# A GEGLU block by seven-product multiplication: one gate/up product of units 6 to 11 divided once more over unit pairs and passes

## Chip, cores, metric

The kernel runs on one core of one Trainium2 chip. The metric is the device time of one execution in microseconds; lower is better. A profile of one execution shows what each engine did: TensorE (PE for its matmuls, PEld for its weight loads), VectorE (DVE), ScalarE (ACT), GpSimd (POOL), and SyncE (SP), which issues the DMAs.

## The reference

```python
# x (1, 2048, 1024), w_gate and w_up (1024, 3584), w_down (3584, 1024), all bfloat16
g = einsum("bsd,df->bsf", x, w_gate)
u = einsum("bsd,df->bsf", x, w_up)
h = gelu(g, approximate=True) * u
return einsum("bsf,fd->bsd", h, w_down)
```

## The kernel before

The 2048 rows of x are worked in two passes (`NPASS`) of two chunks of N = 512 rows. A pass first computes h for its 1024 rows (gate/up stage), then multiplies by `w_down` (`down`). Both products are done by the seven-product scheme of Strassen and Winograd on 2x2 blocks: sums of blocks are formed beforehand, seven block products in place of eight are run on TensorE, and the results are added.

**The gate/up stage** runs over `NU` = 14 units. A unit u holds 256 columns of both `w_gate` and `w_up`, split into two blocks of 128 (fb = 2u and 2u + 1). The contraction of 1024 is split into halves of four blocks of 128 (`KH`), the rows of the pass into the two chunks. The sums of x (`t1` to `t4`, and `tb`, a cast) are made by VectorE once a pass, as fp32r tiles of 128x512. The sums of the weights (`s1` to `s4`) are made by GpSimd in `make_s`, one unit or more ahead of their use; `sa` and `tb` are casts by ScalarE. The seven products of a unit, each for gate and up, each of 4 matmuls of 128x128 by 128x512: two with the raw bf16 weights (`raw_products`, P1 and the one for c11) and five in fp32r, in `unit`: s2 t2, s1 t1, s3 t3, s4 tb and **A22 T4** (`s["sa"]`, `t["t4"]`, last). The raw products of two units are run together near the end of each odd unit, so that TensorE changes between bf16 and fp32r once a pair.

**Banks.** The eight PSUM banks of 128x512 fp32 are used in pairs (gate, up), called E, K, C, F before. The pair e of a unit collects P1, then s2 t2, s3 t3 and A22 T4; between them ScalarE copies its state out (`snap`, p1 and u2). d takes s1 t1 (copied out as p5) and s4 tb. The third pair is scratch: in pass 0 `keep_part` forms there, with ScalarE and VectorE, a part of the sums of `w_down` that the down stage needs (`m`, a pool of one buffer, stored to DRAM by `store_made`). VectorE adds the parts (`add`, `sum`), ScalarE applies `gelu`, VectorE multiplies into `hT` (`times`). `finish_raw` does this for the block that the raw products give.

**Order.** The instructions of SP, VectorE, GpSimd and TensorE, and in these stages of ScalarE, run in program order on each engine; an engine that waits holds up all that stands behind it on that engine. In `unit` the helper `aside` marks places at which other work is put: `aside(0)` stands behind s2 t2 and issues the load of the weights of unit u + 2; `after_p5` (`prepare`) stands behind s1 t1 and its copies, ahead of s3 t3: it makes the next unit's sums on GpSimd, stores the finished `m` and fetches `w_down` rows (`fetch_wd`); `aside(1)` stands ahead of the last additions.

**Buffers.** All small tiles (sums, copies, gelu results, w_down rows) share one pool of 52 slots of 2 KB a partition (`kpool`). The weights of a unit take one of three `w` buffers. The x of a pass takes `xT0` and `xT1`, one buffer each.

All additions appear in the profile under a helper's line: L91 for VectorE (`dve`), L94 for GpSimd (`pool`), L112 for all matmuls; L108 is `snap`, L103 `cast`, L180 `gelu`, L272 the copy in `keep_part`. Names of tiles tell them apart: `m<-bank` is `keep_part`, `sum<-bank,p` and `bank<-bank,p` are the additions of p5 or p1, `sum<-bank,u` those of u2, `hT<-g,bank` is `times`.

Of the kernel before, what the change touches and what calls it, by code (L numbers as in the profile page):

```python
# [10 lines left out]
def kernel(  # L11
# [39 lines left out]
    NKB = Dm // P  # L51
# [31 lines left out]
    def slot(shape, dtype, name):  # L83
        return kpool.tile(shape, dtype, name=name, tag="k")
# [5 lines left out]
    def dve(out, a, b, op):  # L90
        nc.vector.tensor_tensor(out=out, in0=a, in1=b, op=op)  # L91
# [4 lines left out]
    def new(eng, a, b, op, name, shape=None, dtype=None):  # L96
        t = slot(shape or [P, N], dtype or f32r, name)
        eng(t, a, b, op)
        return t

    def cast(src, name, shape=None):
        t = slot(shape or [P, N], f32r, name)
        nc.scalar.copy(out=t, in_=src)  # L103
        return t

    def snap(ps, name):
        t = slot([P, N], f32, name)
        nc.scalar.copy(out=t, in_=ps)  # L108
        return t
# [40 lines left out]
    def sums_s(w, eng):  # L150
        GU = range(2)
        sh = [P, KH, P]
        a11, a21 = [[w[:, i, :KH, h : h + P] for i in GU] for h in (0, P)]
        a12, a22 = [[w[:, i, KH:, h : h + P] for i in GU] for h in (0, P)]
        return Sums(
            how={
                "s1": lambda q, GU=GU: [new(eng, a21[i], a22[i], ADD, "s1", sh) for i in GU],
                "s2": lambda q: [new(eng, q["s1"][i], a11[i], SUB, "s2", sh) for i in GU],
                "s3": lambda q: [new(eng, a11[i], a21[i], SUB, "s3", sh) for i in GU],
                "s4": lambda q: [new(eng, a12[i], q["s2"][i], SUB, "s4", sh) for i in GU],  # L160
                "sa": lambda q: [cast(a22[i], "sa", sh) for i in GU],
            }
        )

    def pool_behind(tile):
        nc.gpsimd.tensor_copy(out=seen, in_=tile[:, :1].bitcast(f32))
# [3 lines left out]
        t.make("t1", "t2", "t3", "tb", "t4")  # L170
        return t

    def make_s(w, eng):
        s = sums_s(w, eng)
        s.make("s1", "s2", "s3", "sa", "s4")
        return s

    def gelu(src):
        g = slot([P, N], f32, "g")
        nc.scalar.activation(g, src, ACT.Gelu_apprx_tanh)  # L180
        return g

    def times(fb, c, g, u):
        dve(hT[:, fb // NJ, fb % NJ, c, :], g, u, MUL)

    def product(ps, lhs, rhs, start):
        for k in range(KH):
            matmul(ps, lhs[:, k, :], rhs[k], start and k == 0, k == KH - 1)

    def raw_products(e, c, xT, w):  # L190
        for i in range(2):
            product(e[i], w[:, i, :KH, :P], [xT[0][:, k, :] for k in range(KH)], True)
        p1 = [snap(e[i], "p1") for i in range(2)]
        for i in range(2):
            b21 = [xT[0][:, KH + k, :] for k in range(KH)]
            product(c[i], w[:, i, KH:, :P], b21, True)
        return p1

    def add(ps, other):
# [4 lines left out]
    def finish_raw(u, c, p1):  # L204
        g, up = add(c, p1)
        times(2 * u, 0, gelu(g), up)

    def unit(u, banks, s, t, late, after_p5, aside, keep, ahead_of_p4, behind_p4):
# [19 lines left out]
        after_p5()  # L228
        for i in GU:
            product(e[i], s["s3"][i], t["t3"], False)  # L230
        g, up = new(dve, e[0], p5[0], ADD, "sum", dtype=f32), banks[1][not late]
        dve(up, e[1], p5[1], ADD)
        if late:
            times(2 * u, 0, *c11)
        for i in GU:
            product(c[i], s["s4"][i], t["tb"], False)
        times(2 * u + 1, 1, gelu(g), up)
        aside(1)
        g, up = add(c, u2)
        times(2 * u, 1, gelu(g), up)  # L240
        ahead_of_p4()
        for i in GU:
            product(e[i], s["sa"][i], t["t4"], False)
        behind_p4()
        times(2 * u + 1, 0, gelu(e[0]), e[1])

    td = dpool.tile([P, NJ, 3, N], f32, name="td")  # L250
    wraw, made = {}, {}

    def fetch_wd(js):
# [381 lines left out]
    E, K, C, F = odd, cc, dd, even  # L635

    def loaded(u):
        if u not in ws:
            ws[u] = load_w(u)
        return ws[u]  # L640

    def raw_of(u, e):
        p1 = raw_products(e, K, xT, loaded(u))
        return lambda: finish_raw(u, K, p1)

    for ip in range(NPASS):
        with tc.manual_schedule(engines={ENG.Activation}):
            if ip == 0:
                ws = {1: w, 2: ahead}
                late = lambda: add(cc, nxt["p1"])  # L650
            else:
                raw_of(0, F)()
                raw_of(1, C)()
            for u in range(1 if ip == 0 else 0, NU):
                js = making(u) if ip == 0 else []
                first = (ip, u) == (0, 1)

                def prepare():
# [23 lines left out]
                def ahead_of_p4():  # L682
                    if u % 2 and u + 1 < NU:
                        raw_of(u + 1, F)()
                        nxt["c11"] = raw_of(u + 2, C)

                def behind_p4():
                    if "c11" in nxt:
                        nxt.pop("c11")()

                if u % 2 and not first:
                    E, K, C = C, E, K
                banks = (E, K, C) if u % 2 else (F, K, E)
                unit(
                    u, banks, s, t, late if first else None, prepare, aside, keep,
                    ahead_of_p4, behind_p4,
                )
                s = nxt.pop("s", None)
# [22 lines left out]
        down(ip, F + K, C + E, last, more)  # L721
        E, K, C, F = K, E, F, C
        if not last:
            t, s = got["t"], got["s"]

# [28 lines left out]
```

## Time and profile before

| | |
|---|---|
| median of 3 runs | 539.94 us (539.25 to 540.3) |
| profiled execution | 539.29 us, span 537.5 us |
| granted TensorE clock, mean | 0.999 |
| TensorE busy | 532.7 us, 2451 matmuls |
| VectorE busy | 356.3 us, 536 instructions |
| ScalarE busy | 258.1 us, 457 instructions |
| GpSimd busy | 259.3 us, 243 instructions |
| the sums of weights on GpSimd, `s<-w` alone | 102 of 1188 ns |

The span is the time from the first to the last instruction of the profiled execution; the execution's own time is 1.8 us longer. Shares of busy time are averages over the whole span, and TensorE's busy time counts its pipelined matmuls from start to end, so the step from one matmul's start to the next says more than a row's duration.

### The profile page before, as it was taken

What the parts mean: (1) busy time and instruction counts of PE and PEld (TensorE: products, weight loads), DVE (VectorE), ACT (ScalarE), POOL (GpSimd) and SP (SyncE); (2) the same over time, 40 slices, a digit from 0 to 9 for tenths busy, and PEclk for the clock granted to TensorE, in tenths of its full rate; (3) what the DMA queues carried; (4) which work ended last, traced back from release to release, by engine and by line L of the source; (5) the groups of instructions that cost most, each with busy time, mean ns of one, the idle gap of its engine ahead of it and who ended that gap; (6) DMA issues with size and microseconds to landing.
All of it is one profiled execution on the core that took longest, in us unless ns stands there. A gap on an engine that the chain in (4) does not pass through costs nothing.

```text
span 537.5 us, 7573 instructions
## 1 busy us (share of the span) xinstructions
PE 532.7 (99%) x2451; PEld 382.4 (71%) x2451; DVE 356.3 (66%) x536; ACT 258.1 (48%) x457; POOL 259.3 (48%) x243
## 2 busy tenths in 40 slices
PE   8999999999999999999999999999999999999997
PEld 4568686867777746888868677776868685478887
DVE  2986766767676894595855464555554639979844
ACT  2556675666666410265355555555555551113340
POOL 1179966677773500000087767676766600000194
PEclk9999999999999999999999999999999999999999
DMA  9675666759482999999873233242520049573752
GB/s 245 156 186 168 186 177 176 218 136 262 131 234 71 383 357 298 308 197 275 264 187 88 78 80 81 77 119 50 145 57 23 2 130 390 204 236 88 243 169 70
DMA packets 108199, 93.30 MB, mean 174 GB/s; under 512 B 17280, under 2 KB 93056, under 8 KB 108160
## 3 DMA queue, kind: packets, MB, share of 16 engines
q1 hardware_dynamic: 108160, 92.82, 59.6%
q8 instruction: 20, 0.33, 0.3%
q14 instruction: 19, 0.16, 0.1%
HBM read 74.45 MB, written 15.20 MB: 167 GB/s over the span
## 4 chain that ended last, share of the span: by engine, by line
PE 98%; DMA 1%; SPq 0%; DVE 0%; issue 0%
PE bank L112 98%; DMA xn<-in_x_dram 1%; SPq L538 0%; DVE st L91 0%; PE bank L545 0%
## 5 line engine op out<-in xcount | busy, mean ns | idle before, releaser
L94 POOL TENSOR_TENSOR s<-w 128x512 fp32r<-128x512 bf16 x102 | 119.0, 1188 | 163.0 <-PE bank L112 113.5
L112 PE MATMUL bank<-t,s 128*128 128x512 f32 x648 | 151.7, 390 | 0.0
L112 PEld LDWEIGHTS bank<-t,s 128*128 128x128 f32 x648 | 121.7, 188 | 25.4
L112 PE MATMUL bank<-xT,w 128*128 128x512 bf16 (+1 forms) x504 | 109.7, 376 | 0.0
L108 ACT COPY p<-bank 128x512 f32<-128x512 f32 x124 | 69.8, 590 | 45.2 <-PE bank L112 45.1
L91 DVE TENSOR_TENSOR sum<-bank,p 128x512 f32<-128x512 f32 x54 | 37.3, 691 | 79.4 <-PE bank L112 78.3
L112 PEld LDWEIGHTS <-w 128*128 128x128 bf16 x504 | 48.1, 98 | 58.1 <-issue 3.4
L91 DVE TENSOR_TENSOR hT<-g,bank 128x512 bf16<-128x512 f32 x112 | 76.8, 688 | 17.6 <-PE bank L112 4.5
L180 ACT ACTIVATE g<-sum 128x512 f32<-128x512 f32 x81 | 51.4, 635 | 74.5 <-DVE sum L91 74.2
L94 POOL TENSOR_TENSOR q<-q 128x256 fp32r<-128x256 f32 x28 | 21.1, 788 | 80.0 <-PE bank L112 79.4
L112 PE MATMUL bank<-q 128*128 128x512 f32 x240 | 59.0, 389 | 0.0
L94 POOL TENSOR_TENSOR s<-w,s 128x512 fp32r<-128x512 bf16 x50 | 57.7, 1175 | 0.0
L94 POOL TENSOR_TENSOR s<-s,w 128x512 fp32r<-128x512 f32 x50 | 57.2, 1166 | 0.0
L112 PE MATMUL bank<-t,sa 128*128 128x512 f32 x216 | 55.9, 401 | 0.0
L112 PE MATMUL bank<-tb,s 128*128 128x512 f32 x216 | 53.3, 389 | 0.0
L108 ACT COPY u<-bank 128x512 f32<-128x512 f32 x62 | 35.5, 589 | 34.3 <-PE bank L112 34.2
L112 PEld LDWEIGHTS bank<-q 128*128 128x128 f32 x240 | 45.1, 188 | 9.3
L112 PE MATMUL bank<-raw,hT 128*128 128x512 bf16 x224 | 48.7, 379 | 0.0
L112 PEld LDWEIGHTS bank<-t,sa 128*128 128x128 f32 x216 | 40.6, 188 | 9.4
L103 ACT CAST tb<-raw 128x512 fp32r<-128x512 bf16 x28 | 17.2, 624 | 62.6 <-DMA raw<-in_w_down_dram 34.1
L112 PEld LDWEIGHTS bank<-tb,s 128*128 128x128 f32 x216 | 40.6, 188 | 8.4
L91 DVE TENSOR_TENSOR bank<-bank,p 128x512 f32<-128x512 f32 x54 | 37.7, 699 | 8.8 <-PE bank L112 6.2
(60 smaller groups left out, 493.8 us busy)
## 6 DMA issues: line engine op xcount, KB each, us to landing
raw<-in_w_down_dram SPq DMA_DIRECT2D x76, 256.0 KB, 5.1
q<-td SPq DMA_DIRECT2D x60, 256.0 KB, 4.9
w<-in_w_gate_dram SPq DMA_DIRECT2D x27, 512.0 KB, 5.9
w<-in_w_up_dram SPq DMA_DIRECT2D x27, 512.0 KB, 7.0
td<-m SPq DMA_DIRECT2D x12, 768.0 KB, 4.6
w<-td SPq DMA_DIRECT2D x6, 1024.0 KB, 10.1
out_dram<-st SPq DMA_DIRECT2D x32, 128.0 KB, 1.7
td<-w SPq DMA_DIRECT2D x2, 768.0 KB, 6.3
```

The source lines that it names most:

```text
L91: nc.vector.tensor_tensor(out=out, in0=a, in1=b, op=op)
L94: nc.gpsimd.tensor_tensor(out=out, in0=a, in1=b, op=op)
L103: nc.scalar.copy(out=t, in_=src)
L108: nc.scalar.copy(out=t, in_=ps)
L112: nc.tensor.matmul(ps, lhsT=lhs, rhs=rhs, start=start, stop=stop, skip_group_check=True)
L180: nc.scalar.activation(g, src, ACT.Gelu_apprx_tanh)
```

## The change

For units 6 to 11, taken as pairs (6, 7), (8, 9), (10, 11) (`SPLIT`), A22 T4 is no longer computed whole in each unit and pass. The A22 of both units of a pair make one matrix, its rows halved by unit and its contraction halved into two blocks of two; the T4 of pass 0 and that of pass 1 make the other. This 2x2 by 2x2 product is done once more by seven products (of 2 x 2 matmuls for gate and up) in place of eight. Five of them run in pass 0, in the odd unit (`split_first`); two of their results are stored to DRAM (`dz`). Two run in pass 1, also in the odd unit (`split_second`), and the stored parts are added there.

What this needs:
- GpSimd makes three extra sums of weights for a pair in each pass (`split_sums`): in pass 0 in the odd unit's `prepare`, ahead of the next unit's sums, in pass 1 in the even unit's, behind them. ScalarE casts A22 only in pass 0 and in the unit itself (`sa` of the even unit, half of it, `sh`, of the odd one).
- T4 of pass 1 has to be there in pass 0. The x of pass 1 is loaded in units 1 and 3 (`NEXT_X`, 16 transposing DMAs in all) into a part of `hT` that is written only from unit 10 on, and VectorE forms 18 sums of 128x512: four times three for T4 (`next_t4`), twice three for the sums of both T4 (`inner_i`). The table `PREP` says how many of them are issued where: "0" at `aside(0)`, "p" at the end of `prepare`, "1" at `aside(1)`. Part of T4 is stored (`di`) and loaded again in unit 1 of pass 1 (`load_i1`).
- The bank pairs get other roles (Ea, Eb, K, D). In a split pair both units keep their e until the end; D is taken three times by half products in pass 0, with copies by ScalarE in between.
- In an odd split unit `up` goes to a slot instead of a bank. `fetch_wd` moves from the end of `prepare` to its beginning, in most split units to `aside(0)`. The raw products of a split pair are issued as two first ones and then two second ones in pass 0.

```diff
+    SPLIT = (6, 8, 10)
+    NEXT_X = {1: (0, 2), 3: (1, 3)}
+    PREP = {(2, "p"): 1, (2, "1"): 1, (3, "0"): 1, (3, "p"): 2, (3, "1"): 1, (4, "0"): 1, (4, "p"): 1, (4, "1"): 1, (5, "0"): 1, (5, "p"): 1, (5, "1"): 2, (6, "0"): 1, (6, "p"): 1, (7, "0"): 1, (7, "p"): 2}
...
+    def split_sums(wa, wb, ip):
+        ka, kb = slice(KH, KH + 2), slice(KH + 2, NKB)
+        a11, a12, a21, a22 = [w[:, :, k, P:] for w in (wa, wb) for k in (ka, kb)]
+        sh = [P, 2, 2, P]
+        q = {"s1": new(pool, a21, a22, ADD, "s1", sh)}
+        q["s2"] = new(pool, q["s1"], a11, SUB, "s2", sh)
+        if ip == 0:
+            q["s3"] = new(pool, a11, a21, SUB, "s3", sh)
+        else:
+            q["s4"] = new(pool, a12, q["s2"], SUB, "s4", sh)
+        return q
...
+    def half(ps, lhs, rhs, start):
+        for i in range(2):
+            for k in range(2):
+                matmul(ps[i], lhs(i, k), rhs[k], start and k == 0, k == 1)
...
+    def split_first(a, ea, eb, z, s, sp, t, c12):
+        sa = s["sa"]
+        half(z, lambda i, k: sa[i][:, k], t["t4"][:2], True)
+        z1 = [snap(z[i], "z1") for i in range(2)]
+        c12()
+        half(ea, lambda i, k: sa[i][:, 2 + k], t["t4"][2:], False)
+        g, up = plus(ea, z1)
+        half(z, lambda i, k: sp["s2"][:, i, k], t["i2"], False)
+        z2 = [snap(z[i], "z2") for i in range(2)]
+        gl = gelu(g)
+        times(2 * a + 1, 0, gl, up)
+        half(eb, lambda i, k: s["sh"][:, i, k], t["i4"], False)
+        half(z, lambda i, k: sp["s3"][:, i, k], t["i3"], False)
+        z3 = [snap(z[i], "z3") for i in range(2)]
+        g, up = plus(eb, z3)
+        for n, zs in enumerate((z2, z3)):
+            for i in range(2):
+                nc.sync.dma_start(out=dz[:, a // 2, n, i], in_=zs[i])
+        times(2 * a + 3, 0, gelu(g), up)
...
+    def split_second(a, ea, y, sp, t, z):
+        half(y, lambda i, k: sp["s1"][:, i, k], t["i1"], True)
+        half(ea, lambda i, k: sp["s4"][:, i, k], t["t4"][2:], False)
+        for n in range(2):
+            for i in range(2):
+                dve(z[n][i], y[i], z[n][i], ADD)
+        g, up = plus(ea, z[0])
+        times(2 * a + 1, 0, gelu(g), up)
...
+    def next_t4(k):
+        lo, hi = [[hT[:, 1, 6 + kk, c, :] for c in range(2)] for kk in (k, KH + k)]
+        def one(t):
+            later[k] = new(dve, lo[1], lo[0], SUB, "t1")
+        def two(t):
+            later[k] = new(dve, hi[1], later[k], SUB, "t2")
+        def three(t):
+            later[k] = new(dve, hi[0], later[k], SUB, "t4")
+        return [one, two, three]
...
                 def prepare():
                     if first:
                         pool_behind(t["t4"][-1])
+                    if ip == 0 and (u == NU - 2 or not apart(u)):
+                        fetch_wd(making(u + 1))
+                    if ip == 0 and odd_u and apart(u):
+                        halves["sp"] = split_sums(ws[u - 1], ws[u], ip)
                     if u + 1 < NU:
-                        nxt["s"] = make_s(loaded(u + 1), pool)
+                        nxt["s"] = make_s(
+                            loaded(u + 1), pool, () if apart(u + 1) else ("sa",)
+                        )
+                        if ip == 1 and not odd_u and apart(u):
+                            halves["sp"] = split_sums(ws[u], ws[u + 1], ip)
+                    if ip == 0 and apart(u):
+                        cast_of = sums_s(ws[u], pool)["how"]
+                        name = "sh" if odd_u else "sa"
+                        halves[name] = cast_of[name](None)
...
-                    if ip == 0:
-                        fetch_wd(making(u + 1))
+                    prep("p")
...
                 def aside(part):
+                    if part >= 0:
+                        prep("01"[part])
...
+                    if part == 0 and ip == 0 and apart(u) and u < NU - 2:
+                        fetch_wd(making(u + 1))
                     if part == 0 and u + 2 < NU:
                         loaded(u + 2)
...
+                    if part == 0 and ip == 0:
+                        for k in NEXT_X.get(u, ()):
+                            next_x(k)
+                    if part == 0 and ip == 1 and u == 1:
+                        load_i1(t)
+                    if part == 1 and ip == 1 and not odd_u and apart(u):
+                        halves["z"] = split_load(u)
...
+                    elif odd_u and ip == 0:
+                        split_first(u - 1, Ea, Eb, D, halves, halves["sp"], t, c12)
+                        p1 = raw_first(K, xT, loaded(u + 1)), raw_first(Ea, xT, loaded(u + 2))
+                        for n, c in enumerate((D, Eb)):
+                            raw_second(c, xT, loaded(u + 1 + n))
+                            finish_raw(u + 1 + n, c, p1[n])
```

More of the change, by code (lines that the diff above doesn't have):

```diff
@@ L206, in finish_raw, with unit @@
         times(2 * u, 0, gelu(g), up)
-    def unit(u, banks, s, t, late, after_p5, aside, keep, ahead_of_p4, behind_p4):
+    def unit(u, banks, s, t, late, after_p5, aside, keep, mid, behind_p7, p4):
         GU = range(2)
@@ L228, in unit @@
         after_p5()
+        mid()
         for i in GU:
             product(e[i], s["s3"][i], t["t3"], False)
-        g, up = new(dve, e[0], p5[0], ADD, "sum", dtype=f32), banks[1][not late]
+        g = new(dve, e[0], p5[0], ADD, "sum", dtype=f32)
+        up = slot([P, N], f32, "up") if apart(u) and u % 2 else banks[1][not late]
         dve(up, e[1], p5[1], ADD)
+        more = behind_p7()
         if late:
@@ L237, in unit, with whole_p4 @@
         times(2 * u + 1, 1, gelu(g), up)
+        if more:
+            times(2 * u + 1, 0, gelu(more[0]), more[1])
         aside(1)
         g, up = add(c, u2)
[L240 to L242 removed]
+        p4(lambda: times(2 * u, 1, gelu(g), up))
+    def whole_p4(u, e, s, t, ahead, behind):
+        ahead()
+        for i in range(2):
             product(e[i], s["sa"][i], t["t4"], False)
[L244 removed]
+        behind()
         times(2 * u + 1, 0, gelu(e[0]), e[1])
+    def half(ps, lhs, rhs, start):
+        for i in range(2):
+            for k in range(2):
+                matmul(ps[i], lhs(i, k), rhs[k], start and k == 0, k == 1)
@@ new lines, in plus @@
+    def plus(ps, other):
+        g = new(dve, ps[0], other[0], ADD, "sum", dtype=f32)
+        dve(ps[1], ps[1], other[1], ADD)
+        return g, ps[1]
+    def split_first(a, ea, eb, z, s, sp, t, c12):
[17 more added lines that the diff above has]
+        times(2 * a + 3, 0, gelu(g), up)
@@ new lines, in split_load @@
+    def split_load(a):
+        z = [[slot([P, N], f32, "z") for i in range(2)] for n in range(2)]
+        for n in range(2):
+            for i in range(2):
+                nc.sync.dma_start(out=z[n][i], in_=dz[:, a // 2, n, i])
+        return z
+    def split_second(a, ea, y, sp, t, z):
+        half(y, lambda i, k: sp["s1"][:, i, k], t["i1"], True)
+        half(ea, lambda i, k: sp["s4"][:, i, k], t["t4"][2:], False)
+        for n in range(2):
+            for i in range(2):
+                dve(z[n][i], y[i], z[n][i], ADD)
+        g, up = plus(ea, z[0])
+        times(2 * a + 1, 0, gelu(g), up)
@@ new lines, in next_x @@
+    def next_x(k):
+        for c in range(2):
+            for kk in (k, KH + k):
+                nc.sync.dma_start_transpose(
+                    out=hT[:, 1, 6 + kk, c, :],
+                    in_=x2[(2 + c) * N : (3 + c) * N, kk * P : (kk + 1) * P],
+                )
[8 more added lines that the diff above has]
+        return [one, two, three]
@@ new lines, in inner_i, with one, two, three @@
+    def inner_i(k):
+        def one(t):
+            if not inner_x:
+                inner_x.append(xpool.tile([P, 4, N], f32r, name="xT1"))
+                t["i2"], t["i3"] = [
+                    [inner_x[0][:, 2 * n + k] for k in range(2)] for n in range(2)
+                ]
+                t["i4"] = []
+            nc.sync.dma_start(out=di[:, k], in_=t["t4"][k].bitcast(f32))
+            dve(t["i3"][k], later[2 + k], later[k], SUB)
+        def two(t):
+            dve(t["i2"][k], t["i3"][k], t["t4"][k], ADD)
+        def three(t):
+            t["i4"].append(new(dve, t["t4"][2 + k], t["i2"][k], SUB, "i4"))
+        return [one, two, three]
@@ L250, with load_i1 @@
+    def load_i1(t):
+        tile = xpool.tile([P, 4, N], f32r, name="xT1")
+        t["i1"] = [tile[:, k] for k in range(2)]
+        for k in range(2):
+            q = slot([P, N], f32, "q")
+            nc.sync.dma_start(out=q, in_=di[:, k])
+            dve(t["i1"][k], t["t4"][k], q, SUB)
+    preps = [
+        op
+        for ops in (next_t4(0), next_t4(2), inner_i(0), next_t4(1), next_t4(3), inner_i(1))
+        for op in ops
+    ]
     td = dpool.tile([P, NJ, 3, N], f32, name="td")
+    di = dpool.tile([P, 2, N], f32, name="di")
@@ L251 @@
+    dz = dpool.tile([P, NU // 2, 2, 2, N], f32, name="dz")
+    later, inner_x = {}, []
     wraw, made = {}, {}
@@ L656 @@
                 first = (ip, u) == (0, 1)
+                odd_u = u % 2 == 1
+                if first or not odd_u:
+                    halves = {}
                 def prepare():
@@ new lines, in mid, with behind_p7, ahead, behind @@
+                def mid():
+                    if ip == 1 and odd_u and apart(u):
+                        split_second(u - 1, Ea, D, halves["sp"], t, halves["z"])
+                def behind_p7():
+                    if ip == 1 and odd_u and apart(u):
+                        return plus(Eb, halves["z"][1])
+                def ahead():
+                    if odd_u and u + 1 < NU:
+                        raw_of(u + 1, Ea, D)()
+                        nxt["c11"] = raw_of(u + 2, K, D)
+                def behind():
@@ L688, in behind_p4, with p4 @@
                     if "c11" in nxt:
                         nxt.pop("c11")()
-                if u % 2 and not first:
-                    E, K, C = C, E, K
-                banks = (E, K, C) if u % 2 else (F, K, E)
+                def p4(c12):
+                    if not (ip == 0 and odd_u and apart(u)):
+                        c12()
+                    if first:
+                        whole_p4(u, odd, s, t, lambda: after_first(), behind)
+                    elif not apart(u):
+                        whole_p4(u, (Ea, Eb)[odd_u], s, t, ahead, behind)
+                    elif odd_u and ip == 0:
[4 more added lines that the diff above has]
+                            finish_raw(u + 1 + n, c, p1[n])
+                    elif odd_u:
+                        p1 = raw_first(Ea, xT, loaded(u + 1))
+                        raw_second(D, xT, loaded(u + 1))
+                        finish_raw(u + 1, D, p1)
+                        p1 = raw_first(Eb, xT, loaded(u + 2))
+                        raw_second(K, xT, loaded(u + 2))
+                        finish_raw(u + 2, K, p1)
@@ L694, with after_first @@
+                def after_first():
+                    raw_of(2, even, cc)()
+                    nxt["c11"] = raw_of(3, dd, cc)
+                if first:
+                    banks = odd, cc, dd
+                else:
+                    banks = (Eb, D, K) if odd_u else (Ea, K, D)
                 unit(
                     u, banks, s, t, late if first else None, prepare, aside, keep,
-                    ahead_of_p4, behind_p4,
+                    mid, behind_p7, p4,
                 )
+                if odd_u and not first and u + 1 < NU:
+                    if not apart(u):
+                        Ea, Eb, K, D = Ea, K, D, Eb
+                    elif ip == 0:
+                        Ea, Eb, K, D = K, Ea, Eb, D
@@ L719, in more @@
                 got["t"] = make_t(xT)
-        down(ip, F + K, C + E, last, more)
-        E, K, C, F = K, E, F, C
+        down(ip, Ea + D, K + Eb, last, more)
+        Ea, Eb, K, D = K, Ea, Eb, D
         if not last:
```

36 lines of the change are left out of this document (21 added, 15 removed).

## The prediction

> **What bounds the kernel now.** I read the page's busy table and chain of waits first, then TensorE's timeline, then VectorE's and GpSimd's timelines around the places where the change puts its new work.
>
> ```profile
> span 537.5 us, 7573 instructions
> ...
> PE 532.7 (99%) x2451; PEld 382.4 (71%) x2451; DVE 356.3 (66%) x536; ACT 258.1 (48%) x457; POOL 259.3 (48%) x243
> ...
> PE 98%; DMA 1%; SPq 0%; DVE 0%; issue 0%
> ```
>
> TensorE is busy for 99% of the span and the chain that ended last is TensorE's own stream for 98% of it; nothing waits inside it. So a matmul taken out is worth its whole step, and so is any wait put in. TensorE's timeline of unit 3 in pass 0 gives the step:
>
> ```profile
> 49.72 5.60 PE L112 MATMUL bank<-t,s 128*128 128x512 f32 x24
> 55.16 1.98 PE L112 MATMUL bank<-tb,s 128*128 128x512 f32 x8
> 56.98 7.08 PE L112 MATMUL bank<-xT,w 128*128 128x512 bf16 x32
> 63.71 2.19 PE L112 MATMUL bank<-t,sa 128*128 128x512 f32 x8
> ```
>
> From start to start, 24 fp32r matmuls take 55.16 - 49.72 = 5.44 us, 0.227 each; the 32 bf16 ones 0.216 each (6.91 to the first fp32r one, whose recorded start is early by one weight load). Below, S is the start of an odd unit (49.72 here).
>
> VectorE is the engine behind, by its timeline in the same unit (start, duration, what it does, idle before it):
>
> ```profile
> 52.12 0.69 DVE L91 TENSOR_TENSOR m<-bank,raw 128x512 fp32r<-128x512 f32 x1 [1.44 <-ACT bank L272]
> 53.61 1.49 DVE L91 TENSOR_TENSOR m<-bank,m 128x512 fp32r<-128x512 f32 x2 [0.80 <-ACT bank L272]
> 55.01 0.68 DVE L91 TENSOR_TENSOR sum<-bank,p 128x512 f32<-128x512 f32 x1
> ...
> 58.74 0.69 DVE L91 TENSOR_TENSOR hT<-g,bank 128x512 bf16<-128x512 f32 x1
> 59.85 0.69 DVE L91 TENSOR_TENSOR sum<-bank,p 128x512 f32<-128x512 f32 x1 [0.42 <-PE bank L112]
> ...
> 61.52 0.69 DVE L91 TENSOR_TENSOR hT<-g,bank 128x512 bf16<-128x512 f32 x1
> ```
>
> The last row empties the bank pair into which TensorE's last eight raw matmuls go next: its second bank is due at 56.98 + 28 x 0.216 = 63.03, and the row ends at 62.21. VectorE has 0.8 us there, and 0.5 more because the row at 59.85 waited 0.42 for TensorE.
>
> **The saving.** A22 T4 now costs 16 matmuls in each pass for a pair of units. After the change pass 0 has five half products of 4 matmuls (20) and pass 1 two (8): 28 in place of 32, over three pairs 12 fewer. 12 x 0.227 = 2.72 us off, wholly on the path. The number of switches between bf16 and fp32r stays, and the halves have the same 128x512 shape, so each keeps its 0.227.
>
> **The bank chain of the half products.** In pass 0 the pair D takes three half products in turn, each copied out by ScalarE (0.59 us a copy, 0.51 from start to start when they queue). A consumer starts 0.28 us after the last matmul's slot ends (59.85 against 59.57 for its bank). The first copy thus runs from 0.73 to 1.32 after the half product's start, the second to 1.83; TensorE comes back to the banks at 1.82 and 2.27, with four matmuls on another pair between. Margin 0.34 to 0.5, if ScalarE is free: cost 0, and up to 0.3 us a visit (two visits, three pairs: 1.8 us) if it is not. In pass 1 the new VectorE work of a pair (four additions of the stored parts, four more into banks: eight at 0.60) ends in my chain some 0.6 us before the tightest bank is due; VectorE is busy there for 11.86 of 23.10 us, so I take 0.
>
> **GpSimd, loads, stores.** GpSimd gets three more sums a pair, 3 x 1.16 us, in both passes: 16 + 3 = 19 ops, 22 us of the pair's 26.0 in pass 0 and of 23.3 in pass 1. It works a unit ahead today: the sums for unit 6 end at 78.70 and are first used at 90.81. I take 0. The z stores (four of 256 KB a pair) and loads, the 16 transposing loads of the next x (1.13 to 1.26 us each on SP's queue, landing 2.5 to 5.8 us after issue) and the earlier w_down loads have units of time ahead of their readers: 0. ScalarE makes six z copies a pair in place of one A22 cast in pass 0, and four fewer casts in pass 1: 0.
>
> **The 18 sums of x.** These are new on VectorE in units 2 to 7: in program order they stand before work that frees banks. Unhindered each costs 0.60 (the step of queued rows above). Units 2 and 3 hold two and four of them. Three lie ahead of unit 3's first row above. VectorE is free for them at 50.6, less some 0.6 of gaps in unit 2 that they fill, so that row would start at 50.0 + 1.8 = 51.8, no later than now (its w_down rows, which hold it to 52.12 today, are now loaded earlier). Then come two behind "m" and one ahead of the unit's second pair of additions. The row of 59.85 becomes 54.7 (end of "m": 51.8, a ScalarE copy, two rows) - 0.1 + 1.2 + 4.33 (today's way from 55.01 to 58.74 + 0.60) + 0.6 = 60.7, against a latest time of 60.9 (63.03 less 2.15 for sum, gelu and product). So at 0.60 each they just fit, with 0.2 us to spare, and every tenth that one of them takes beyond that is added six times.
>
> They will take more, since both of their inputs lie in SBUF and GpSimd works at the same time. The last down stage has the only overlap of the two kinds, in VectorE's and GpSimd's timelines:
>
> ```profile
> 506.90 0.68 DVE L91 TENSOR_TENSOR q<-raw 128x512 fp32r<-128x512 bf16 x1
> 507.50 1.22 DVE L91 TENSOR_TENSOR q<-hT,q 128x512 fp32r<-128x512 bf16 x1
> 508.65 1.22 DVE L91 TENSOR_TENSOR q<-hT 128x512 fp32r<-128x512 bf16 x1
> ```
>
> ```profile
> 507.30 2.03 POOL L94 TENSOR_TENSOR q<-q 128x256 fp32r<-128x256 f32 x2 [78.79 <-PE bank L112]
> ```
>
> Beside a GpSimd op VectorE's 0.69 becomes 1.22: 0.54 of waiting behind an op that takes 0.74. The other way round, before pass 1:
>
> ```profile
> 270.04 2.50 DVE L91 TENSOR_TENSOR t<-xT,t 128x512 fp32r<-128x512 bf16 x4
> ```
>
> ```profile
> 270.35 4.30 POOL L94 TENSOR_TENSOR s<-w 128x512 fp32r<-128x512 bf16 x2 [86.06 <-PE bank L112]
> ```
>
> Here four queued VectorE sums kept their step (2.50 for four) and GpSimd's first op stretched to 3.2 us. The ordinary VectorE rows read one operand from a bank and show no such stretch beside GpSimd. [...]
>
> A GpSimd op here is 1.16 us long and steps by 1.12, so by the same measure it holds VectorE off for about 1.0. A sum that comes at a random moment then waits between 0 and 1.0, on average 0.45 while GpSimd runs without a gap; the second of two waits 0 (270 us) to 1.0 (508 us), I take half. GpSimd is busy throughout 40.7 to 65.9 (25.2 of 25.2 us by the windows) and for 18.5 of 25.0 us in units 4 and 5 (0.74).
> - Units 2 and 3: 5 x 0.45 + 0.5 - 0.2 = 2.55 us of stall.
> - Units 4 and 5 (six that count, the one at the start of unit 4 fills a gap of 1.6): 5 x 0.33 + 0.37 - 0.2 = 1.8.
> - Units 6 and 7: four count; the way is wider, some 0.85 to the first z copy: 3 x 0.33 + 0.37 - 0.85 = 0.5.
>
> Sum 4.85 us, between 0 and (all six at 1.0, twice, and four: 5.8 + 5.8 + 3.15) 14.75; the mean wait in it is 0.38. Where VectorE is late, the product that frees the D banks is late next, and TensorE waits for it at its last raw products.
>
> **Sum.** -2.72 + 4.85 = +2.1 us: 539.29 becomes 541.4 for the profiled execution (span 537.5 and 1.8 around it), which lies 0.65 below the median of the runs shown; 542.0 as the median.
>
> **Rivals.**
> - **The sums find their gaps** (not slower). GpSimd has idle stretches of 3.0 to 3.9 us a unit from 66.6 on, waiting for slots; the new tiles take slots, so it may pause more and be out of the way, and queued sums may pass it as at 270 us. It decides at a mean wait of 0.25 us a sum: 16 counted sums x 0.25 less 1.25 us of room are the 2.7 us saved. With no waits: 539.94 - 2.72 = 537.2. For it: at 0.60 all fits. Against: no idle time at all on GpSimd in units 2 and 3. Chance 0.32 for a gain that can be measured, 0.10 for a draw (stalls of 1.6 to 3.8 us).
> - **The third w buffer.** A pair's weights are now held until GpSimd's three extra sums in the odd unit, and the load for unit u + 2 waits for that buffer. It is needed at S + 7.26 + 4.54 + 1.73 = S + 13.5 and takes 5.9 us to land, so GpSimd must be done by S + 7.6. If it starts its odd unit's work as late as in unit 5 (82.24, S + 7.4), it ends at S + 10.9: 3.3 us a pair, 9.9 - 2.7 = +7.2: 547.1. Against: it is a unit ahead. Chance 0.06.
> - My forecast, slower through the port: 0.52.
>
> **Numbers.** A measurement of this kernel tells about 0.2% (1.08 us) from no change. Faster 0.32, same 0.10, slower 0.58. The low end, 536.9, takes in no stall at all; the high end, 545.5, a mean wait of 0.6 (16 x 0.6 - 1.25 - 2.72 = +5.6). The forecast's own range is 541.1 (0.2% slower) to 545.5.
>
> **What would show it.** Right: 2439 matmuls; "later" and "t" sums of VectorE at 0.9 to 1.7 us instead of 0.69; GpSimd ops of 1.7 in units 2 to 7; TensorE gaps of 0.3 to 1 us at the raw products of units 3 and 5 and at the first half products of unit 7, released by VectorE, and none in units 8 to 11 or in pass 1. Wrong: these sums at 0.69 and a TensorE without gaps (537.2), or gaps before the raw products of units 7, 9 and 11 that end with a w load.

## The result, and the profile after

The changed kernel takes 545.51 us (median of four executions, 545.46 to 545.61) against 539.60 for the kernel before on the same chip: a ratio of 1.0112, 95% interval 1.0099 to 1.0125. It is slower, by 5.9 us where 2.1 were forecast, and just above the range. The profiled execution has a span of 543.7 us.

The page of the changed kernel, its busy table and its chain of waits:

```profile
span 543.7 us, 7662 instructions
...
PE 532.3 (98%) x2418; PEld 380.2 (70%) x2439; DVE 398.4 (73%) x592; ACT 257.5 (47%) x460; POOL 287.4 (53%) x261
...
PE 92%; DVE 4%; issue 2%; ACT 1%; DVEq 0%; ACTq 0%
```

The 2439 weight loads are those of the 2439 matmuls that were foreseen (some matmul records are missing). The chain is no longer TensorE alone: 4% of it is VectorE. TensorE's timeline of units 2 and 3 (start, duration, what it does, idle before it and who ended that) shows where:

```profile
46.00 1.98 PE L115 MATMUL bank<-tb,s 128*128 128x512 f32 x8
49.71 2.14 PE L115 MATMUL bank<-t,sa 128*128 128x512 f32 x8 [1.73 <-DVE sum L94]
51.69 5.93 PE L115 MATMUL bank<-t,s 128*128 128x512 f32 x24
58.80 2.09 PE L115 MATMUL bank<-tb,s 128*128 128x512 f32 x8 [1.19 <-ACT p L111]
60.96 4.47 PE L115 MATMUL bank<-xT,w 128*128 128x512 bf16 x19
65.86 1.89 PE L115 MATMUL bank<-xT,w 128*128 128x512 bf16 x8 [0.42 <-DVE hT L94]
67.90 1.02 PE L115 MATMUL bank<-xT,w 128*128 128x512 bf16 x4 [0.16 <-DVE hT L94]
```

The last two gaps are those foreseen, at unit 3's raw products. The first two, larger, were not. VectorE's timeline there, and GpSimd's below it:

```profile
43.74 1.49 DVE L94 TENSOR_TENSOR m<-bank,m 128x512 fp32r<-128x512 f32 x2 [1.62 <-ACT bank L402]
45.15 3.91 DVE L94 TENSOR_TENSOR t<-hT 128x512 fp32r<-128x512 bf16 x1
48.98 0.68 DVE L94 TENSOR_TENSOR sum<-bank,p 128x512 f32<-128x512 f32 x1
...
50.97 1.60 DVE L94 TENSOR_TENSOR t<-hT,t 128x512 fp32r<-128x512 bf16 x1
...
55.14 1.26 DVE L94 TENSOR_TENSOR t<-hT,t 128x512 fp32r<-128x512 bf16 x1
```

```profile
43.96 2.29 POOL L97 TENSOR_TENSOR s<-w 128x512 fp32r<-128x512 bf16 x2
46.22 2.28 POOL L97 TENSOR_TENSOR s<-w,s 128x512 fp32r<-128x512 bf16 x2
49.73 2.29 POOL L97 TENSOR_TENSOR s<-w 128x512 fp32r<-128x512 bf16 x2 [1.23 <-DVE sum L94]
...
54.70 2.73 POOL L97 TENSOR_TENSOR s<-w 128x512 fp32r<-128x512 bf16 x2
```

The first of the 18 sums takes 3.91 us. It started 0.06 us after a GpSimd instruction and ended 0.56 us after the third one (48.50), when GpSimd stopped to wait for VectorE itself (`<-DVE sum`). The instructions behind it, which free the bank that TensorE wants at 47.8 (eight steps of 0.227 behind 46.00), are late with it. The later sums wait for one GpSimd instruction: the sum at 55.14 started 0.44 us after one of 54.70 and took 1.26; the one at 50.97, 0.10 us after the second one of the row at 49.73, took 1.60. Delay and duration add up to 1.70 in both, so each of these GpSimd instructions of 1.16 us held VectorE off for its first 1.0 us; and the next GpSimd instruction then took 1.6 (2.73 for the two at 54.70).

Unit 7 is the other place. VectorE, then ScalarE, then TensorE:

```profile
109.71 1.17 DVE L94 TENSOR_TENSOR xT<-xT,t 128x512 fp32r<-128x512 f32 x1
110.91 1.54 DVE L94 TENSOR_TENSOR i<-t,xT 128x512 fp32r<-128x512 f32 x1
112.37 0.68 DVE L94 TENSOR_TENSOR sum<-bank,p 128x512 f32<-128x512 f32 x1
...
113.75 1.38 DVE L94 TENSOR_TENSOR hT<-g,up 128x512 bf16<-128x512 f32 x1
```

```profile
113.08 0.63 ACT L196 ACTIVATE g<-sum 128x512 f32<-128x512 f32 x1 [2.77 <-DVE sum L94]
113.62 1.06 ACT L111 COPY z<-bank 128x512 f32<-128x512 f32 x2
```

```profile
111.37 1.98 PE L115 MATMUL bank<-t,sa 128*128 128x512 f32 x8
114.33 1.17 PE L115 MATMUL bank<-xT,s 128*128 128x512 f32 x4 [0.99 <-ACT z L111]
```

Two sums put the addition at 112.37 back, the gelu behind it on ScalarE starts at 113.08, and the copies of the first half product stand behind that gelu: TensorE comes back to the banks and waits. The product `hT<-g,up` is new in this role: in the odd split units `up` lies in a slot, so this instruction too has two SBUF inputs, and it took 1.38 us.

### The profile page after: what moved, and what is told of

Same layout as the page of the kernel before. It is cut to its first block, busy times and chain, and to the rows that moved or that the text cites. A ratio compares the mean times of both kernels' runs of the same rounds, so it can differ in the third digit from the quotient of the medians.

```text
span 543.7 us, 7662 instructions
## 1 busy us (share of the span) xinstructions
PE 532.3 (98%) x2418; PEld 380.2 (70%) x2439; DVE 398.4 (73%) x592; ACT 257.5 (47%) x460; POOL 287.4 (53%) x261
## 4 chain that ended last, share of the span: by engine, by line
PE 92%; DVE 4%; issue 2%; ACT 1%; DVEq 0%; ACTq 0%
PE bank L115 91%; DVE sum L94 1%; DVE hT L94 1%; ACT g L196 1%; DVE t L94 1%; DVE m L94 1%; PE bank L730 1%; PE bank L675 1%; DVE xT L94 0%; ACT bank L402 0%; DVE st L94 0%; ACT z L111 0%; DVEq L94 0%; ACTq L196 0%; DVE i L94 0%
## 5 line engine op out<-in xcount | busy, mean ns | idle before, releaser
L97 POOL TENSOR_TENSOR s<-w 128x512 fp32r<-128x512 bf16 x111 | 132.7, 1215 | 155.8 <-PE bank L115 121.5
L115 PE MATMUL bank<-t,s 128*128 128x512 f32 x660 | 156.6, 392 | 0.1
L115 PEld LDWEIGHTS bank<-t,s 128*128 128x128 f32 x660 | 123.8, 188 | 27.1 <-issue 0.4
L196 ACT ACTIVATE g<-sum 128x512 f32<-128x512 f32 x93 | 58.8, 633 | 101.8 <-DVE sum L94 101.3
L94 DVE TENSOR_TENSOR hT<-g,bank 128x512 bf16<-128x512 f32 x106 | 72.4, 687 | 14.2 <-ACT g L196 3.6
L97 POOL TENSOR_TENSOR s<-s,w 128x512 fp32r<-128x512 f32 x56 | 65.6, 1190 | 0.5
L97 POOL TENSOR_TENSOR s<-w,s 128x512 fp32r<-128x512 bf16 x53 | 63.9, 1225 | 0.2
L94 DVE TENSOR_TENSOR q<-hT 128x512 fp32r<-128x512 bf16 x56 | 38.9, 695 | 5.8 <-PE bank L115 5.8
L115 PEld LDWEIGHTS <-hT 128*128 128x128 bf16 x224 | 21.8, 98 | 26.4 <-issue 0.5
L115 PE MATMUL bank<-t,sa 128*128 128x512 f32 x144 | 37.0, 399 | 1.7 <-DVE sum L94 1.7
```

The costliest lines, as they stand in the source:

```text
L97: nc.gpsimd.tensor_tensor(out=out, in0=a, in1=b, op=op)
L115: nc.tensor.matmul(ps, lhsT=lhs, rhs=rhs, start=start, stop=stop, skip_group_check=True)
```

## Where the time went, interval by interval

The table takes each kernel's TensorE timeline from one raw-product stage to the next (units 1 to 3, 3 to 5, 5 to 7), us. In the third, units 6 and 7 are divided, which costs 0.91 us of extra matmuls and moves the raw products behind the half products, so 27.64, its length in `e12`, stands for the one without a stall: `e12`, told last, has no gap of TensorE in any of the three. Intervals are from the profiled execution, times are medians.

| kernel | time, us | first VectorE sum | 1 to 3 | 3 to 5 | 5 to 7 |
|---|---|---|---|---|---|
| before | 539.6 | none | 25.10 | 25.08 | 25.08 (not divided) |
| changed | 545.5 | 3.91 | 28.93 | 26.19 | 30.93 |
| e1_no_sums | 536.9 | none | 25.08 | 25.08 | 28.37 |
| e3_no_reads | 538.0 | 0.68 | 25.08 | 25.08 | 28.07 |
| e6_first_moved | 548.9 | 7.59 | 32.57 | 25.54 | 31.19 |
| e11_moved_pause | 542.2 | 0.85 | 25.10 | 26.91 | 30.93 |
| e10_gaps_pause | 538.4 | 0.68 | 25.08 | 25.57 | 28.29 |
| e12_in_place | 537.6 | 0.68 | 25.08 | 25.08 | 27.64 |

The changed kernel loses 3.85 + 1.11 + 3.29 = 8.25 us here, and nothing in units 8 to 11 (26.07 a pair in it and in e12 alike). In pass 1 a divided pair takes 23.32 in place of 25.08.

## Experiments

**Sums, order, or the rest.** Three theories, by the letters that the expectations use: P, the exclusion between GpSimd's sums and VectorE's sums with two SBUF inputs; O, the sums' own 0.60 us in program order; S, loads, slots and the divided units themselves. Four kernels tell them apart. The first leaves the sums out:

```diff
     def next_t4(k):
...
-        return [one, two, three]
+        return [lambda t: None] * 3
     def inner_i(k):
...
-        return [one, two, three]
+        return [one] + [lambda t: None] * 2
```

> Left out: the 18 sums of x in units 2 to 7 of pass 0 (other tiles stand in for their results); the loads of x, the store of t4, the z stores and loads, the slots and the half products all stay. Theory P (VectorE's sums with two SBUF inputs and GpSimd's sums keep each other out): the stalls of units 2 to 5 are gone and most of unit 7's, 537.0 to 538.2 us. Theory O (the sums' own 0.60 us each, in program order ahead of what frees banks, is too much by itself; GpSimd has no part in it): the same, 537.0 to 538.2. Theory S (loads, stores, slots, w buffers or the half products' bank chain): at least 541, with the gaps of units 3 and 7 still there.

Measured: 536.92 us, ratio 0.9962 (0.9949 to 0.9974). S falls: without the sums the rest of the change gains. Two intervals are clean; the third is 0.73 too long, and one instruction alone is late ahead of that gap. VectorE, then GpSimd, of this kernel:

```profile
104.92 2.88 DVE L94 TENSOR_TENSOR hT<-g,up 128x512 bf16<-128x512 f32 x1
```

```profile
104.92 2.33 POOL L97 TENSOR_TENSOR s<-w,s 128x512 fp32r<-128x512 bf16 x2
```

The product with `up` in a slot was kept out through both GpSimd instructions of that row.

The second has the sums and no divided units:

```diff
-    SPLIT = (6, 8, 10)
+    SPLIT = ()
```

> The other part alone: x is loaded and summed as in the changed kernel, but no pair of units is divided (32 matmuls of A22 T4 a pair, as before; the results of the sums are not used). Theories P and O: the stalls of units 2 to 5 stay (5.6 us) and nothing is saved; in units 6 and 7 there is no half product to be late, so 0 to 2.6: 545.2 to 548.0 us. Theory S, if it is the divided units: 539.5 to 541; if it is the loads of x: 545 as well.

Measured: 545.50 us, ratio 1.0115 (1.0100 to 1.0130). The sums alone cost 6.3 us; the first took 3.90 in the same place.

The third takes GpSimd's reading away. (Its memsets are also shorter, 0.53 us in place of 1.16, so GpSimd is idle for most of the time here.)

```diff
+    fills = []
...
     def pool(out, a, b, op):
-        nc.gpsimd.tensor_tensor(out=out, in0=a, in1=b, op=op)
+        if fills:
+            nc.gpsimd.memset(out.bitcast(f32), 0.0)
+        else:
+            nc.gpsimd.tensor_tensor(out=out, in0=a, in1=b, op=op)
...
+                    if ip == 0 and u <= 7:
+                        fills.append(u)
...
+                    fills.clear()
```

> Left out: GpSimd's sums of weights that it makes in units 1 to 7 of pass 0 are memsets of the same tiles, which write SBUF and read nothing; all else, the 18 sums of x on VectorE too, is as in the changed kernel. Theory P: the sums of x go back from 0.7 to 3.9 us to 0.69 each, the gaps of units 2 to 5 go: 537 to 539 us. Theory O: the sums still stand in the way, 544.5 to 546. Theory S: 544.5 to 546, less if GpSimd's shorter work frees slots earlier.

Measured: 537.99 us, ratio 0.9977 (0.9967 to 0.9987). VectorE's sums, at the same places in its order, and GpSimd beside them:

```profile
45.47 0.68 DVE L94 TENSOR_TENSOR t<-hT 128x512 fp32r<-128x512 bf16 x1
...
48.06 0.69 DVE L94 TENSOR_TENSOR t<-hT,t 128x512 fp32r<-128x512 bf16 x1
```

```profile
46.81 1.66 POOL L100 MEMSET s<- 128x512 f32 x3 [5.92 <-DVE sum L94]
```

Every sum is back at 0.68 or 0.69, and so are the four that started while a memset ran (at 48.06, 51.31, 76.29 and 100.58). O falls: at their own cost the sums fit in units 2 to 5 without any gap, as the prediction had worked out, and make unit 7 late by 0.43. P stands: beside GpSimd's sums they took up to 3.91 us in the changed kernel, those four beside memsets, which read nothing, 0.69 at most.

The fourth moves the sums to where GpSimd has pauses:

```diff
-    SPLIT = (6, 8, 10)
+    SPLIT = (8, 10)
-    PREP = {(2, "p"): 1, (2, "1"): 1, (3, "0"): 1, ...
+    PREP = {(4, "0"): 1, (4, "p"): 1, (4, "1"): 1, ...
```

> The same 18 sums on VectorE in units 4 to 9 (7, 7 and 4 a pair) in place of 2 to 7, where GpSimd has idle stretches; for that only units 8 to 11 are divided (8 matmuls fewer than before, 1.8 us saved). Theory P: mean wait of a sum 0.3 or less, stalls of 1 to 3 us: 539 to 541.5. Theory O: a sum costs as much anywhere, about 0.46 us of stall each as in the changed kernel, 8.2 in all: 546. Theory S: 541 to 545.

Measured: 542.82 us, ratio 1.0067 (1.0052 to 1.0082). Above what P gave and far below O's 546; it lies in the range of S, which e1 rules out. The sums waited 0.3 us on average, as taken (5.8 us in all over 18), but more of that reached TensorE than the 1 to 3 us expected. No sum was kept out for more than one GpSimd instruction; the first of them met the last one before a pause and took 1.60 us.

**What the 3.91 is.** It alone exceeds the 1.0 us that the prediction had as the worst wait of a sum. Three more kernels first tried the sums in other places: `e5_in_gaps` puts 8 ahead of instructions at which VectorE waits anyway and gives 10 to GpSimd; `e6_first_moved` moves only the first; `e7_waits_only` keeps 18 on VectorE in its waiting places.

```diff
                 def keep(part, ps):
...
+                    if part == 0:
+                        prep("k")
...
                 def ahead():
+                    if not first:
+                        prep("r")
...
+    a, b, c, d = next_t4(0, dve), next_t4(2, pool), next_t4(1, pool), next_t4(3, pool)
+    preps = a[:2] + b + c[:2] + a[2:] + i[:1] + c[2:] + d[:1] + i[1:2] + d[1:] + i[2:] + j
```

> All the work of the changed kernel, with the 18 sums elsewhere: 8 stay on VectorE, each ahead of an instruction that waits there anyway (behind the first keep subtraction of the even units, 1.6 us; ahead of the first one of the odd units, 1.1 to 1.5; ahead of the first sum of the raw products of units 3 and 5, 1.1), 10 go to GpSimd behind its weight sums of units 3 (5), 4 (2), 5 (2) and 6 (1), where it was idle for 6.3, 2.6, 3.3 and 1.7 us. Theory P with the unhindered cost hidden: units 2 to 5 without a gap, in unit 7 only what the product hT<-g,up loses (0 to 1): 537.2 to 538.5 us. If GpSimd's added sums delay the weights (rival): gaps at the start of units 4 to 7, 540 to 543.

Measured: no single time. Of ten executions five took 536.8 to 538.3 us and five 543.0 to 545.0; the ratio is 1.002 (0.998 to 1.0061). The profile is of the fastest, and its first sum took 1.40. The five longer ones had a granted clock of 0.993 to 0.996, the others 0.999 or 1.000; clocks of that size go with a long wait in the profiles of e6, e7 and e9 below (0.994, 0.994 and 0.993), but none of e5's longer executions was profiled.

```diff
-    PREP = {(2, "p"): 1, (2, "1"): 1, ...
+    PREP = {(2, "0"): 1, (2, "1"): 1, ...
```

> The changed kernel with one of the 18 sums moved: the first, which took 3.91 us, goes from behind the keep subtractions of unit 2 to ahead of them, where VectorE waits 1.6 us for ScalarE. If three GpSimd instructions in a row kept it out by an accident of its start (0.05 us after one of theirs), it takes 0.7 to 1.7 us here and the gap of 2.1 us at 47.6 goes: 542.3 to 543.5 us. If any two-input sum in GpSimd's unbroken run of units 2 and 3 is kept out to the run's end: 545 to 546.

Measured: 548.94 us, with one execution at 542.55 and three at 548.5 to 549.8; ratio 1.0146 (1.0087 to 1.0204). Both expectations missed. VectorE, GpSimd and TensorE in the profile:

```profile
41.79 7.59 DVE L94 TENSOR_TENSOR t<-hT 128x512 fp32r<-128x512 bf16 x1
49.31 0.68 DVE L94 TENSOR_TENSOR m<-bank,raw 128x512 fp32r<-128x512 f32 x1
```

```profile
42.08 2.28 POOL L97 TENSOR_TENSOR s<-s,w 128x512 fp32r<-128x512 f32 x2
44.32 2.28 POOL L97 TENSOR_TENSOR s<-w 128x512 fp32r<-128x512 bf16 x2
46.57 2.26 POOL L97 TENSOR_TENSOR s<-w,s 128x512 fp32r<-128x512 bf16 x2
52.80 2.27 POOL L97 TENSOR_TENSOR s<-w 128x512 fp32r<-128x512 bf16 x2 [3.97 <-DVE sum L94]
```

```profile
51.78 3.75 PE L115 MATMUL bank<-tb,s 128*128 128x512 f32 x8 [5.26 <-ACT p L111]
```

The first sum was kept out by seven GpSimd instructions in a row, to the end of the run. Every later sum of this kernel waited for one instruction at most (the next two took 1.29 and 1.35). So it isn't the place, and not the moment of the start (0.06 us after a GpSimd start before, 0.85 here). The last row shows a second price: after 5.26 us of idleness eight matmuls took 3.75 us in place of 1.98.

```diff
-    PREP = {(2, "p"): 1, (2, "1"): 1, (3, "0"): 1, ...
+    PREP = {(2, "k"): 1, (3, "0"): 2, (3, "k"): 1, ...
```

> The changed kernel with all 18 sums on VectorE, but each placed ahead of an instruction that waits there anyway (7 in units 2 and 3, 7 in 4 and 5, 4 in 6 and 7; the waits are 0.4 to 1.6 us long), GpSimd's work unchanged. If what costs is a sum of up to 1.7 us in a place with less room: 539 to 541 us, with small gaps where the wait was 0.4 to 0.8. If a sum costs the same anywhere on VectorE: 545.

Measured: 542.00 us, between the two expectations, nine executions from 540.6 to 546.3; ratio 1.0054 (1.0029 to 1.0080). In its profile, of one at 546.0, the first sum took 7.13 (six GpSimd instructions), the others 0.7 to 1.7.

In every profile with a long wait it is the first VectorE instruction with two SBUF inputs that comes upon a running GpSimd: the first sum in the changed kernel, e2, e6 and e7, and `hT<-g,up` in e1. That became theory K, against L, a matter of that one place. The next kernel gives the first sum to GpSimd:

```diff
         def one(t):
-            later[k] = new(dve, lo[1], lo[0], SUB, "t1")
+            later[k] = new(dve if k else pool, lo[1], lo[0], SUB, "t1")
```

> The changed kernel with the first of the 18 sums, the one that took 3.91 us, made by GpSimd behind its weight sums of unit 2; the other 17 stay on VectorE. Theory K (the first VectorE sum with two SBUF inputs that meets a running GpSimd is kept out until GpSimd pauses, whichever sum it is and wherever it stands; later ones wait for the end of one GpSimd instruction): the second sum, which took 1.60 us behind the first, now takes 2.5 us or more, and the time is 544 to 549 us. Theory L (the long wait belongs to that one place): all 17 take 0.7 to 1.7 us, 542 to 543.5 us.

Measured: 551.64 us, ratio 1.0225 (1.0208 to 1.0242), beyond K's 544 to 549 and nowhere near L. VectorE, GpSimd, TensorE:

```profile
49.47 8.31 DVE L94 TENSOR_TENSOR t<-hT,t 128x512 fp32r<-128x512 bf16 x1 [1.90 <-POOL t L97]
```

```profile
56.06 1.17 POOL L97 TENSOR_TENSOR s<-w,s 128x512 fp32r<-128x512 bf16 x1
59.25 1.16 POOL L97 TENSOR_TENSOR s<-w,s 128x512 fp32r<-128x512 bf16 x1 [2.01 <-ACT g L196]
```

```profile
60.74 3.75 PE L115 MATMUL bank<-t,s 128*128 128x512 f32 x8 [7.50 <-ACT u L111]
```

The second sum, 1.60 us in the changed kernel, is now the first to meet GpSimd and takes 8.31: it gets in when GpSimd, at 57.23, stops for 2.0 us.

If K is right, a pause of GpSimd at the first sum cures it. One instruction makes one; `e11_moved_pause` is e6 with this edit, `e10_gaps_pause` is e5 with it:

```diff
         s = sums_s(w, eng)
-        s.make("s1", "s2", "s3", *casts, "s4")
+        s.make("s1")
+        if later and not paused:
+            paused.append(pool_behind(later[0]))
+        s.make("s2", "s3", *casts, "s4")
...
-    later, inner_x = {}, []
+    later, inner_x, paused = {}, [], []
```

> e6_first_moved, whose first sum was kept out for 7.59 us in its profile and whose runs were 542.6 and 548.5 to 549.8 us, with the same pause of GpSimd behind its first two weight sums of unit 2. Theory K: the first sum takes 0.7 to 1.7 us in every execution; 542 to 543.5 us in all runs, which is the changed kernel less the 2 to 3 us that its first sum lost. Theory L: 548 to 550, as without the pause.

Measured: 542.24 us (542.1 to 543.6), ratio 1.0050 (1.0035 to 1.0065), against 548.94 without the pause. The first sum took 0.85, and the next, in the middle of an unbroken GpSimd run, 1.05.

> e5_in_gaps, whose runs lay between 536.8 and 545.0 us, with one instruction more: behind its first two weight sums of unit 2 GpSimd copies one column of the first sum of x, so it pauses until VectorE has made that sum. Theory K: the first sum gets in at that pause in every execution (0.7 to 1.7 us), later sums wait for one GpSimd instruction each, and all runs lie at 536.5 to 538.5 us. Theory L, or a cause other than GpSimd for the spread: the runs still lie between 537 and 545.

Measured: 538.40 us, all ten executions from 537.9 to 539.7; ratio 0.9982 (0.9973 to 0.9991). The group of e5 above 543 is gone, as K had it; five of the ten lie above K's 538.5. GpSimd, then VectorE:

```profile
39.81 2.29 POOL L97 TENSOR_TENSOR s<-w 128x512 fp32r<-128x512 bf16 x2
42.75 0.18 POOL L170 COPY seen<-t 128x1 f32<-128x1 f32 x1 [0.65 <-DVE t L94]
42.89 2.30 POOL L97 TENSOR_TENSOR s<-s,w 128x512 fp32r<-128x512 f32 x2
```

```profile
42.00 0.68 DVE L94 TENSOR_TENSOR t<-hT 128x512 fp32r<-128x512 bf16 x1
```

GpSimd gives up 0.65 us and VectorE gets in at once.

**A version that beats both.** It is e10 with two small edits:

```diff
-    PREP = {... (6, "p"): 1, (7, "0"): 1}
+    PREP = {... (6, "p"): 2}
...
         def two(t):
-            later[k] = new(eng, hi[1], later[k], SUB, "t2")
+            eng(later[k], hi[1], later[k], SUB)
         def three(t):
-            later[k] = new(eng, hi[0], later[k], SUB, "t4")
+            eng(later[k], hi[0], later[k], SUB)
...
-            t["i4"].append(new(dve, t["t4"][2 + k], t["i2"][k], SUB, "i4"))
+            t["i4"].append(new((dve, pool)[k], t["t4"][2 + k], t["i2"][k], SUB, "i4"))
```

> e10_gaps_pause with two small edits where its profile still shows TensorE waiting, 0.5 us at 62.7 and 0.5 at 103.6: the t4 sums are made in place (8 buffers fewer taken, since at 62.7 a gelu of ScalarE waited 2.6 us for a buffer that a GpSimd sum still read), and the last sum, which stood on VectorE ahead of the first keep subtraction of unit 7 and took 1.6 us there, goes to GpSimd behind its weight sums of unit 6. Theory K with nothing left in the way: 537.0 to 538.0 us in all runs, faster than before by 0.3 to 0.5%. Rival: GpSimd, which no longer has idle time, is now late with the weights of units 7 and 8: 538.5 to 540.

Measured: 537.59 us (537.3 to 538.1), ratio 0.9966 (0.9952 to 0.9979). Its page:

```profile
span 536.3 us, 7671 instructions
...
PE 530.0 (99%) x2418; PEld 380.5 (71%) x2439; DVE 388.0 (72%) x581; ACT 258.5 (48%) x460; POOL 298.6 (56%) x273
...
PE 96%; DMA 3%; issue 0%; SPq 0%; DVE 0%
```

VectorE is out of the chain again, and the three intervals hold no stall. All the work of the change is in it.

## Why the prediction was wrong, step by step

- **The 18 sums of x**, the step that failed, by size. Its mechanism (VectorE's sums and GpSimd's keep each other out) is shown by e3, where all of them take 0.68 or 0.69 us without GpSimd's sums, and so is its claim that the sums fit at 0.60 each in units 2 to 5. No run shows the port that the prediction names beside its chance of 0.52; the runs show waits, in the changed kernel 3.2 us for the first sum and 0 to 0.9 for the others. What was mis-sized:
  - *Units 2 and 3*: 2.55 forecast, 3.85 + 1.11 = 4.96 measured. The bound of 1.0 us a wait was false for the first sum, which waited 3.2. With that one wait taken out (e11, which also moves the sum, as e6 does) the two units lose 0.02 + 1.83 = 1.85 in place of 4.96, and the kernel takes 542.24 in place of 545.51, next to the 542.0 on record. That one wait is thus worth 3.1 us by the table and 3.3 by the times, of the 3.5 by which the forecast missed.
  - *Units 4 and 5*: 1.8 forecast, 0.7 measured (TensorE's gaps at unit 5's raw products). GpSimd was idle or just ending for most of the sums: 1.4 us of waits in place of 2.0, and more room than taken.
  - *Units 6 and 7*: 0.5 forecast, 2.6 measured (3.29 less those 0.7). The room of 0.85 us was not there: with every sum at 0.69 (e3) the third interval is still 0.43 longer than in e12. And `hT<-g,up` was left out of the sum: it turned into an instruction with two SBUF inputs on the same path, and lost 0.70.
  - So the agreement of e11 with the forecast is partly two errors that cancel, 4.85 against 1.85 + 0.7 + 2.6 = 5.15 by different parts.
- **The saving**: right in TensorE's stream. A divided pair takes 23.32 in place of 25.08 in pass 1 (8 matmuls, 1.8 us) and 26.07 in place of 25.08 in pass 0. Over three pairs that is 3 x (25.08 + 25.08 - 26.07 - 23.32) = 2.3 us in place of 2.72; and 8.25 us of stalls less 2.3 are the 5.9 that were measured. With the stalls gone e12 gains 1.8; the rest is lost in small steps that no run isolated.
- **The bank chain of the half products**: 0 holds in units 9 and 11 and everywhere in e12, but the step had "if ScalarE is free": in unit 7 its copies stood behind a gelu that VectorE's sums had made late, which is part of the 2.6.
- **GpSimd, loads, stores**, and the rival of the **third w buffer**: right, no gap ends with a load of weights, and e1 carries all these transfers at 536.92.
- The rival in which **the sums find their gaps** did not happen in this order of work; e12 shows that it can be arranged.

## What to carry to other kernels

Before putting a sum of two SBUF tiles on VectorE beside a GpSimd that works without pause, look at what stands behind it on VectorE: the waits (here about 1.0 us or less behind one GpSimd instruction, 2.2 to 7.6 behind a run of them), not the 0.6 us, are its price. Give GpSimd a pause at the first such sum, by one tiny instruction that reads its result (0.18 us behind 0.65 of idleness in e10, where the sum took 0.68), and put the others where VectorE waits anyway or on GpSimd itself. And when a buffer moves from a bank to SBUF, check which instructions thereby get a second SBUF input: `hT<-g,up` took 1.38 us in unit 7 of the changed kernel and 2.88 in e1, `hT<-g,bank` 0.69.

## What was not expected of the hardware

- **The first contender can be kept out for a whole run.** In the six profiles with a long wait it was the first VectorE instruction with two SBUF inputs to meet a running GpSimd: 2.88, 3.90, 3.91, 7.13, 7.59 and 8.31 us; those of e1, the changed kernel, e7, e6 and e9 ended 0.55 or 0.56 us after the last GpSimd instruction before a pause. All later ones in the same kernels, up to the end of the span, waited for about one (1.66 us at most in the changed kernel, 1.7 in e7). It is not a fixed rule, so K is shown as a risk and its cure, not as a law: the first sum of e5's profile got in after one instruction (1.40 us), and e5's executions fell into two groups; in the kernel before, the sum at 507.50 (in the prediction), the first to wait for GpSimd there, did so too (1.22). In e12 the first sum ran in the pause and met no GpSimd; the second, the first to meet one, got in within one instruction, in the middle of a run. VectorE, then GpSimd:

```profile
50.76 0.92 DVE L94 TENSOR_TENSOR t<-hT,t 128x512 fp32r<-128x512 bf16 x1
```

```profile
49.97 2.74 POOL L97 TENSOR_TENSOR s<-w 128x512 fp32r<-128x512 bf16 x2
```

  The later waits, about 1.0 us or less, are for one GpSimd instruction, the long ones for two to seven. Why these differ stays open.
- **A long stall cost twice.** The granted clock of TensorE, from the table by windows (third column from the end), in e6 after 5.26 us of idleness, and below it in the changed kernel after 1.73:

```profile
51.70:55.70 4.00, 3.92 (x9) 3.14 (x10) 3.60 (x6) 1.99 (x4) 2.90 (x3) 0.50 0.72 188
```

```profile
49.70:53.00 3.30, 3.29 (x14) 2.71 (x15) 3.20 (x4) 0.62 (x1) 3.27 (x3) 1.00 1.52 261
```

In e6 the eight matmuls behind the wait took 3.75 - 1.98 = 1.8 us longer at this clock, and in e9 too (3.75 us after 7.50 of idleness, the clock at 0.50 from 60.7 to 64.3), the two kernels whose first contender was kept out longest; after the changed kernel's 1.73 us the clock stayed at 1.00. In e7, after 3.24 us of idleness, the clock was at 0.50 as well, and still so in the next 3 us:

```profile
51.60:54.00 2.40, 2.40 (x6) 1.92 (x7) 2.30 (x4) 0.97 (x2) 1.72 (x2) 0.50 1.00 274
54.00:57.00 3.00, 3.00 (x9) 2.32 (x8) 2.35 (x4) 1.23 (x3) 3.00 (x4) 0.50 1.04 280
```
